# A chunked recurrence with a feed-forward block behind it: taking the four batches side by side

## The chip, the cores and the metric

The kernel runs on one core of a Trainium2 chip. A core has a matrix engine (TensorE, PE in the profile; its weight loads are listed apart as PEld), a vector engine (VectorE, DVE), a scalar engine (ScalarE, ACT), a general engine (GpSimd, POOL) and a sync engine (SyncE, SP), which here only issues DMAs. Each engine takes its own list of instructions; semaphores make one wait for another. The metric is the device time in microseconds of one execution. Lower is better.

## What is computed

```python
f = 1.0 / (1.0 + np.exp(-f_logit))              # B, H, S, D = 4, 8, 768, 48
state = np.zeros((B, H, D, D))
for t in range(S):
    state = f[:, :, t, :, None] * state + np.einsum('bhd,bhe->bhde', k[:, :, t], v[:, :, t])
    y[:, :, t] = np.einsum('bhd,bhde->bhe', q[:, :, t], state)
x = y.transpose(0, 2, 1, 3).reshape(B * S, H * D)   # 3072 x 384
a, b = x @ w1, x @ w2                                # w1, w2: 384 x 1024
out = (a * b @ w3) @ w_out                           # w3: 1024 x 1024, w_out: 1024 x 384
```

A gated linear recurrence runs over 768 tokens for each of 4 batches and 8 heads. Its output, with the heads side by side, goes through a feed-forward block whose hidden layer is the product of two projections. The four weight matrices come as 64-bit floats and have to be turned into 32-bit floats on the core.

## The kernel before

**The recurrence.** The tokens are cut into chunks of 128, so there are NU = 24 chunks, NCH = 6 for each batch. Two heads share the 112 used partitions (rows 0 to 47 and 64 to 111), and four such pairs (HP = 4) lie along the free axis. For a chunk u the function `front` loads q, k, the gate's logits and v, takes the sigmoid (`gates`, L518, ScalarE), and forms two running products of the gates on VectorE: `forward` (L526) and, after a reciprocal of the ends (L536), `backward` (L548). They scale q and k (`scale_q` L542, `scale_k` L556). `last` (L531) keeps the forward product's last column. Then, on TensorE, `turn` (L593) transposes the scaled k, copied to the tile kt by ScalarE (L727), and `pairs` forms the products of keys and queries. ScalarE copies them to the tile A (L700, L703), POOL zeroes what lies above the diagonal (`causal`, L709), `values` multiplies with v, and `update` forms the chunk's own contribution to the state from kt and v.

There are two forms. The first NPE = 2 chunks are taken whole: `pairs` with 128 by 128 blocks (L569), `first_values` (L607), and the contribution of the chunk before from a block-diagonal copy of the state (`blocks`, L834, and L613), and `first_update` (L625). All later chunks are cut into halves of 64 tokens: `pairs` with 64 by 64 blocks (L579), `values` (L653), `update` (L686). There a state in the middle, "mid", is wanted: `middle` adds the first half's contribution to the state S of the chunk before (L759), and the second half's to that (L762). `from_state` (L672) then multiplies q with S for the first half and with mid for the second. Before S is read by the next chunk, `state` scales it (L818, for the first two chunks L822 to L825) with G, the product of the chunk's last column and the next chunk's first gate, which POOL forms (`gains`, L809). A chunk that opens a batch (u = 0, 6, 12, 18) has no S to read, a chunk that closes one (5, 11, 17, 23) leaves out the second half of its update.

On TensorE the parts of a chunk are one task: for chunks 2 and 3 `begin` (pairs and update) and a "visit" (values and from_state); from chunk 4 on, the visit of u also holds pairs and update of u + 1. The output ys (L845) goes into the feed-forward block's input xt: for the first NPE chunks through TensorE (`moved`, L874) and ScalarE (L879), later with two DMAs through DRAM (yt, then xt: L866, L869).

**The weights.** `fetch` loads a piece of a matrix as pairs of 32-bit words into the tile "place" (L1396); ScalarE turns the lower words into a number (L1400), VectorE shifts the upper words (L1415), merges the two (L1419) and joins them (L1425). w1 and w2 come in four quarters, by the string EARLY = "23ACBD", which is the order on VectorE after chunk 1: chunks 2 and 3, then A (w1, first half of the hidden units), C (w1, second half), B (w2, first half) and D (w2, second half). Then come w_out and the rows of w3, and `fold` (L1464) forms w3 times w_out.

**The feed-forward block.** The tokens are taken in six blocks of 512, each of the four chunks 4n to 4n + 3. The first block's up projections (`part`, L897) run in groups of three matmuls over 256 tokens (six instructions in the trace); later blocks use a scheme with seven products instead of eight (`seven`, L993) or a longer one (`many`, L1148). `down` (L897 too, by a helper) multiplies with the folded weights and stores rows of the output (L1318). A line such as L897 is that of a helper that several parts call.

**What sets the order.** All of this is written as tasks with an engine, a cost, what they depend on, and a priority, into a `Plan`. `listed` takes, again and again, the task that can begin first by these costs, and the instructions are emitted in that order. So a changed dependency or a changed cost can move tasks on all engines and all DMA issues. `idle` (L399) puts matmuls on a constant tile where the plan expects TensorE to wait in the first 130 us. SP's list is in the plan too: a DMA that has to wait for its buffer holds back those behind it. The v tiles come from a pool of three (chunk 3 has a place of its own), so v of chunk 4 waits for chunk 0, v of chunk 5 for chunk 1.

The lines of the old kernel that the change touches most, the reading of the state:

```python
        for half in range(2):
            state = s["mid"] if half else st[u - 1].get("S")
            if state is None or half == 0 and u % NCH == 0:
                continue
```

Of the kernel before, what the change touches and what calls it, by code (L numbers as in the profile page):

```python
# [36 lines left out]
F32 = mybir.dt.float32  # L37
# [23 lines left out]
NPE = 2  # L61
# [226 lines left out]

def rows(par):
    return slice(64 * par, 64 * par + D)  # L290
# [3 lines left out]
def ranged(ctx, tc, q, k, f_logit, v, w1, w2, w3, w_out, out, ident, w12, wc, left):  # L294
# [30 lines left out]
    sb = [t[0:R, 0 : HP * R].rearrange("p (h r) -> p h r", r=R) for t in firsts]  # L325
# [80 lines left out]
    def setup():  # L406
# [21 lines left out]
        for t in sb:  # L428
            nc.vector.memset(t, 0.0)
# [43 lines left out]
    def loaded(dst, u):  # L473

        nc.sync.dma_start(dst, v[u])

    def front(u):
# [6 lines left out]
        def load(dst, src):  # L484
            def emit():
                if dst is fs[0] and u == 0:

                    nc.sync.dma_start(dst[0:64], src[u].rearrange("two d n -> (two d) n")[0:64])
                    nc.sync.dma_start(dst[rows(1)], src[u, 1])
                    return  # L490
                for par in range(2):
                    nc.sync.dma_start(dst[rows(par)], src[u, par])
            return emit
# [26 lines left out]
        t["g"] = plan.add("ACT", 0.65, gates, [t["lf"]] + past(u, 2, "r") + past(u, 3, "G"), n0)  # L520
        if u % NCH and "G" in tk[u - 1]:
            tk[u - 1]["G"]["deps"].append(t["g"])
# [75 lines left out]
    def first_values(u):  # L598

        s = st[u]  # L600
        opens = u % NCH == 0
        s["yb"] = bank().rearrange("p (h c) -> p h c", c=C)[0:R]
        for hp in range(HP):
            for par in range(2):
# [4 lines left out]
                    rhs=s["A"][:, par, hp], start=hp == 0, stop=opens, skip_group_check=True,  # L609
                )  # L610
        if not opens:
            for hp in range(HP):
                nc.tensor.matmul(  # L613
                    s["yb"][:, hp], lhsT=sb[(u - 1) % 2][:, hp], rhs=s["Q"][:, hp * C : hp * C + C],
                    start=False, stop=True, skip_group_check=True,
                )
# [44 lines left out]
    def from_state(u):  # L661

        s = st[u]
        for half in range(2):
            state = s["mid"] if half else st[u - 1].get("S")
            if state is None or half == 0 and u % NCH == 0:
                continue
# [9 lines left out]
    def update(u):  # L677
# [3 lines left out]
        for hp in range(HP):  # L681
            for half in range(1 if u % NCH == NCH - 1 else 2):
# [38 lines left out]
    def turning(u):  # L721
# [7 lines left out]
        if u < NPE:  # L729
            t["t"] = plan.add("PE", 0.45, lambda: turn(u), [t["k"]] + past(u, 1, "d"), need(u) - 999)  # L730
# [6 lines left out]
    def begin(u):  # L737

        def emit():
# [5 lines left out]
            "PE", 1.1, emit, [t["q"], t["k"], t["e"], t["lv"]] + past(u, 1, "m", "d"), need(u) - 999, slack=0.8,  # L745
# [3 lines left out]
    def middle(u):  # L749

        s, t = st[u], tk[u]
        opens, closes = u % NCH == 0, u % NCH == NCH - 1

        def emit():
            s["mid"] = mids[u % 2]
            if opens:
                nc.vector.tensor_copy(s["mid"], s["pd"][0])
            else:
                nc.vector.tensor_tensor(s["mid"], s["pd"][0], st[u - 1]["S"], ALU.add)  # L759
            if not closes:  # L760
                s["S"] = work.tile([R, HP, D], F32, name="S")
# [3 lines left out]
            "DVE", 0.36 if closes else 0.72, emit, [t["s"], t["m"]] + ([] if opens else past(u, 1, "d")) + past(u, 2, "v"), need(u) - 5,  # L765
        )

    def rest(u):
        s, t = st[u], tk[u]
        opens, closes = u % NCH == 0, u % NCH == NCH - 1  # L770
        n0 = need(u)
        if u < NPE:
# [5 lines left out]
                "PE", 1.05 if opens else 2.1, lambda: first_values(u), [t["c"], t["lv"]] + past(u, 1, "b"), n0 - 998,  # L778
                takes=["f"],
            )  # L780
            t["s"] = plan.add("PE", 0.6, lambda: first_update(u), [t["e"], t["lv"]] + past(u, 1, "d"), n0 - 997)
        else:
# [4 lines left out]
            def visit():  # L787
# [11 lines left out]
                [t["c"], t["lv"], t["mid"]] + past(u, 1, "y", *([] if opens else ["d"])) + [after[nm] for nm in ("q", "k", "e", "lv") if after],  # L799
# [6 lines left out]
        if not closes:  # L806
            def gains():
                s["G"] = work.tile([R, HP], F32, name="G")
                nc.gpsimd.tensor_tensor(s["G"], lasts[:, u], heads(gate[(u + 1) % 2][:, 0:NQ])[:, :, 0], ALU.mult)  # L809

            t["G"] = plan.add(
                "POOL", 0.3, gains, [t["l"]] + [tk[u + 1][nm] for nm in "g" if nm in tk[u + 1]] + past(u, 2, "d"), n0,
            )

            def state():
                gain = s["G"].unsqueeze(2).to_broadcast([R, HP, D])
                if u >= NPE:
                    nc.vector.tensor_tensor(s["S"], s["S"], gain, ALU.mult)  # L818
                    return
                s["S"] = work.tile([R, HP, D], F32, name="S")  # L820
                if opens:
                    nc.vector.tensor_tensor(s["S"], s["pd"], gain, ALU.mult)  # L822
                else:
                    nc.vector.tensor_tensor(s["S"], s["pd"], st[u - 1]["S"], ALU.add)
                    nc.vector.tensor_tensor(s["S"], s["S"], gain, ALU.mult)  # L825

            t["d"] = plan.add(
                "DVE", 0.36 if opens or u >= NPE else 0.72, state,
                [t["s"], t["G"]] + (past(u, 2, "b") if u < NPE else [t["mid"]]), n0, shared=True,
            )  # L830

            def blocks():
                for par in range(2):
                    nc.scalar.copy(sb[u % 2][rows(par), :, 64 * par : 64 * par + D], s["S"][rows(par)])  # L834

            if u + 1 < NPE:
                t["b"] = plan.add("ACT", 0.75, blocks, [t["d"]] + past(u, 1, "v"), n0)
# [23 lines left out]
        def written():  # L861

            s["yt"] = dram.tile([DM, C], F32, name="yt")
            for half in range(2):
                to = s["yt"][half * DH : half * DH + DH].rearrange("(b d) c -> d b c", d=D)
# [1145 lines left out]
```

## The time and the profile before

| | us |
|---|---|
| median of 3 runs (462.68 to 463.16) | 462.83 |
| the profiled execution | 464.25 |
| its span, from the first instruction to the last | 462.5 |
| ScalarE, GpSimd busy | 208.6, 63.9 |
| TensorE's granted clock over the span | 1.000 |

Engine busy time in stretches of the span (us; TensorE, weight loads, VectorE, ScalarE, GpSimd, and the mean busy share of the DMA engines):

| stretch | PE | PEld | DVE | ACT | POOL | DMA |
|---|---|---|---|---|---|---|
| 0 to 20 | 16.73 | 13.40 | 17.27 | 9.62 | 14.77 | 0.70 |
| 20 to 40 | 19.68 | 16.98 | 18.21 | 12.36 | 3.86 | 0.93 |
| 60 to 70 | 10.00 | 8.33 | 9.14 | 3.97 | 0.00 | 1.00 |
| 100 to 150 | 50.00 | 41.64 | 45.66 | 14.84 | 11.05 | 0.40 |
| 200 to 250 | 49.88 | 46.07 | 40.50 | 17.20 | 12.51 | 0.41 |
| 400 to 450 | 50.00 | 47.33 | 31.57 | 16.50 | 0.00 | 0.10 |

How to read it: a row of the timeline gives the start in the span, the duration, the engine, the line of the kernel, the operation, the tile that is written and those that are read, and in brackets how long the engine was idle before it and what ended that. "Waits" lists who waited for whom: total, times, longest. Busy TensorE time includes the filling matmuls of L399. Matmuls are pipelined and their ends are modelled, so the distance between starts says more than a duration.

### The profile page before, as it was taken

What the parts mean: (1) busy time and instruction counts of PE and PEld (TensorE: products, weight loads), DVE (VectorE), ACT (ScalarE), POOL (GpSimd) and SP (SyncE); (2) the same over time, 40 slices, a digit from 0 to 9 for tenths busy, and PEclk for the clock granted to TensorE, in tenths of its full rate; (3) what the DMA queues carried; (4) which work ended last, traced back from release to release, by engine and by line L of the source; (5) the groups of instructions that cost most, each with busy time, mean ns of one, the idle gap of its engine ahead of it and who ended that gap; (6) DMA issues with size and microseconds to landing.
All of it is one profiled execution on the core that took longest, in us unless ns stands there. A gap on an engine that the chain in (4) does not pass through costs nothing.

```text
span 462.5 us, 11749 instructions
## 1 busy us (share of the span) xinstructions
PE 452.9 (98%) x4800; PEld 395.5 (86%) x4800; DVE 362.1 (78%) x633; ACT 208.6 (45%) x468; POOL 63.9 (14%) x90
## 2 busy tenths in 40 slices
PE   7999999999999999999999999999999999999995
PEld 6788885666899888888998888998898988889995
DVE  8988899999898999988973599885658566768441
ACT  4565343432233553443323356566675666672000
POOL 9330000211223432223222000000000000000000
PEclk9999999999999999999999999999999999999999
DMA  6896997833246764447324337653265523200111
GB/s 181 272 331 206 336 353 254 267 104 103 70 125 178 213 185 125 111 124 191 102 55 114 112 94 216 201 157 125 95 184 170 192 69 96 89 1 0 35 69 39
DMA packets 43309, 68.75 MB, mean 149 GB/s; under 512 B 5217, under 2 KB 28386, under 8 KB 42226
## 3 DMA queue, kind: packets, MB, share of 16 engines
q1 hardware_dynamic: 43250, 67.95, 47.8%
q8 instruction: 39, 0.64, 0.6%
q14 instruction: 20, 0.16, 0.1%
HBM read 58.88 MB, written 9.04 MB: 147 GB/s over the span
## 4 chain that ended last, share of the span: by engine, by line
PE 94%; POOL 2%; DVE 2%; issue 0%; POOLq 0%; DVEq 0%
PE f L897 25%; PE f L993 15%; PE f L1148 11%; PE f L1464 9%; PE py L1148 6%; PE pa L1148 5%; PE py L897 4%; PE pa L897 4%; PE py L653 3%; PE pa L579 2%; PE pa L686 2%; PE f L593 2%; PE py L672 2%; PE py L993 1%; POOL ab L437 1%; PE f L399 1%
## 5 line engine op out<-in xcount | busy, mean ns | idle before, releaser
L709 POOL TENSOR_SCALAR_AFFINE_SELECT A<-A 64x512 f32<-64x512 f32 (+1 forms) x46 | 42.3, 920 | 110.6 <-ACT A L703 108.5
L1464 PE MATMUL f<-place 128*128 128x384 f32 x128 | 42.4, 487 | 0.0
L897 PE MATMUL f<-xt,w 128*128 128x256 f32 x192 | 42.1, 380 | 0.0
L897 PEld LDWEIGHTS f<-xt,w 128*128 128x128 f32 x192 | 36.3, 190 | 5.0
L1464 PEld LDWEIGHTS f<-place 128*128 128x128 f32 x128 | 23.9, 190 | 15.5
L993 PE MATMUL f<-xt,w 128*128 128x256 f32 x140 | 36.2, 380 | 0.0
L897 PE MATMUL f<-place 128*128 128x192 f32 x192 | 34.8, 327 | 0.0
L897 PEld LDWEIGHTS f<-place 128*128 128x128 f32 x192 | 31.5, 190 | 0.3 <-issue 0.2
L548 DVE TENSOR_TENSOR_SCAN bwd<-gate,back 112x512 f32<-112x512 f32 x24 | 30.4, 1268 | 0.7
L526 DVE TENSOR_TENSOR_SCAN fwd<-gate,floor 112x512 f32<-112x512 f32 x24 | 30.0, 1251 | 1.2 <-ACT gate L518 0.3
L993 PEld LDWEIGHTS f<-xt,w 128*128 128x128 f32 x140 | 26.3, 190 | 3.5
L845 ACT ACTIVATE ys<-py 112x512 f32<-112x512 f32 x22 | 13.1, 596 | 32.7 <-PE py L672 28.1
L1400 ACT ACTIVATE place<-place 128x512 f32<-128x512 uint32 (+2 forms) x24 | 21.3, 888 | 9.1 <-DMA place<-in_w_dram 7.9
L897 PE MATMUL f<-wc,ab 128*128 128x192 f32 x128 | 23.6, 328 | 0.0
L993 PE MATMUL f<-place 128*128 128x256 f32 x84 | 22.4, 385 | 0.0
L897 PEld LDWEIGHTS f<-wc,ab 128*128 128x128 f32 x128 | 21.3, 190 | 0.4
L518 ACT ACTIVATE gate<-f 112x512 f32<-112x512 f32 x22 | 13.9, 632 | 17.0 <-DMA f<-in_f_logit_dram 7.9
L809 POOL TENSOR_TENSOR G<-lasts,gate 112x4 f32<-112x4 f32 x20 | 11.0, 549 | 76.4 <-ACT lasts L531 30.4
L653 PEld LDWEIGHTS py<-A,vt 64*64 64x64 f32 (+1 forms) x672 | 13.3, 127 | 7.3 <-issue 6.5
L653 PE MATMUL py<-A,vt 64*64 64x64 f32 (+1 forms) x672 | 18.1, 223 | 0.2
L1540 ACT ACTIVATE A<-A,back 128x512 f32<-128x512 f32 x23 | 17.9, 778 | 0.2
L1262 DVE TENSOR_TENSOR place<-ab 128x512 f32<-128x512 f32 x24 | 16.5, 689 | 1.0 <-PE f L897 0.9
(355 smaller groups left out, 1045.6 us busy)
## 6 DMA issues: line engine op xcount, KB each, us to landing
place<-in_w_dram SPq DMA_DIRECT2D x21, 512.0 KB, 6.1
A<-in_w_dram SPq DMA_DIRECT2D x19, 512.0 KB, 4.1
place<-in_w_dram SPq DMA_DIRECT2D x8, 1024.0 KB, 5.9
q<-in_q_dram SPq DMA_DIRECT2D x46, 96.0 KB, 2.6
vt<-in_v_dram SPq DMA_DIRECT2D x23, 192.0 KB, 3.1
out_dram<-o SPq DMA_DIRECT2D x23, 192.0 KB, 2.1
k<-in_k_dram SPq DMA_DIRECT2D x44, 96.0 KB, 2.4
yt<-ys SPq DMA_DIRECT2D x44, 96.0 KB, 2.9
```

Source lines behind the costliest of these rows:

```text
L518: nc.scalar.activation(gate[u % 2][:, 0:NQ], fu, AF.Sigmoid)
L526: nc.vector.tensor_tensor_scan(s["P"], gate[u % 2][:, 0:NQ], floor, 0.0, ALU.mult, ALU.max)
L548: nc.vector.tensor_tensor_scan(s["R"][:, ::-1], gate[u % 2][:, NQ:0:-1], back[:, ::-1], 0.0, ALU.mult, ALU.max)
L653: done = nc.tensor.matmul(y_block(u, hp, par, half)[p0 : p0 + w], lhsT=s["v"][half * W : half * W + W, h * D : h * D + w], rhs=s["A"][half ...
L709: nc.gpsimd.affine_select(out=a, in_=a, pattern=pattern, compare_op=ALU.is_ge, fill=0.0, base=0, channel_multiplier=-1,)
L897: nc.tensor.matmul(out_, lhsT=lhs[i], rhs=rhs[i], start=start and i == 0, stop=i == len(lhs) - 1, skip_group_check=True,)
L993: nc.tensor.matmul(q[nm][:, which * TH : which * TH + TH], lhsT=lhs[i](which), rhs=rhs[i], start=start and which == 0 and i == 0, stop=i = ...
L1148: nc.tensor.matmul(banks[g, c][:, which * TH : which * TH + TH], lhsT=lhs, rhs=x_node(a), start=first and which == 0, stop=True, skip_grou ...
L1262: nc.vector.tensor_tensor(abs_[j], x, y, op)
L1400: nc.scalar.activation(part_.bitcast(F32), part_, AF.Copy, bias=2.0, scale=2.0**-51)
L1464: nc.tensor.matmul(w3s["p", jc], lhsT=w3s[jc][:, kc * P : kc * P + P], rhs=wos[:, kc], start=(kc == 0), stop=(kc == KF - 1),)
L1540: return lambda: nc.scalar.activation(a, a, AF.Sign, bias=small, accum_out=counts[:, i : i + 1])
```

## The change

The number u of a chunk no longer runs through one batch after the other. With `chunk(u) = u % B * NCH + u // B` the chunks 0 to 3 are the first of the four batches, 4 to 7 the second, and so on. The loads take `chunk(u)`, the stores take the rows that belong to it; a block of the feed-forward part now holds one chunk of each batch. So the state that chunk u reads is that of u - 4: five tiles for states go round (three of their own, two in unused columns of A), and G of u uses the gate of u + 4. The chunks that open a batch are 0 to 3, those that close one 20 to 23.

NPE becomes 4: the four opening chunks are all taken whole, so none has a state in the middle, at token 64. Since none of them reads a state, the block-diagonal copies with their clearing and the matmuls on them go. The contribution of an opening chunk is copied to its state by ScalarE (`saved`); the scaling of S, now the same for all chunks, waits for that copy. The number of chunks that go to xt through TensorE stays at two by a constant of its own, MOVED; chunks 2 and 3 go through DRAM as before, with the order of the heads in the whole form.

```diff
-NPE = 2
+NPE = 4
+MOVED = 2
...
+def chunk(u):
+
+    return u % B * NCH + u // B
...
-    sb = [t[0:R, 0 : HP * R].rearrange("p (h r) -> p h r", r=R) for t in firsts]
+    states = [keep.tile([R, HP, D], F32, name=f"S{i}") for i in range(3)]
+    states += [t[0:R, 2 * HP * W + HP * D : 2 * HP * W + 2 * HP * D].rearrange("p (h d) -> p h d", d=D) for t in flat]
...
-        for t in sb:
-            nc.vector.memset(t, 0.0)
...
-        nc.sync.dma_start(dst, v[u])
+        nc.sync.dma_start(dst, v[chunk(u)])
...
-        t["g"] = plan.add("ACT", 0.65, gates, [t["lf"]] + past(u, 2, "r") + past(u, 3, "G"), n0)
-        if u % NCH and "G" in tk[u - 1]:
-            tk[u - 1]["G"]["deps"].append(t["g"])
+        t["g"] = plan.add("ACT", 0.65, gates, [t["lf"]] + past(u, 2, "r") + past(u, B + 2, "G"), n0)
+        if u >= B and "G" in tk[u - B]:
+            tk[u - B]["G"]["deps"].append(t["g"])
...
-                    rhs=s["A"][:, par, hp], start=hp == 0, stop=opens, skip_group_check=True,
-                )
-        if not opens:
-            for hp in range(HP):
-                nc.tensor.matmul(
-                    s["yb"][:, hp], lhsT=sb[(u - 1) % 2][:, hp], rhs=s["Q"][:, hp * C : hp * C + C],
-                    start=False, stop=True, skip_group_check=True,
+                    rhs=s["A"][:, par, hp], start=hp == 0, stop=True, skip_group_check=True,
                 )
...
-            state = s["mid"] if half else st[u - 1].get("S")
-            if state is None or half == 0 and u % NCH == 0:
+            state = s["mid"] if half else st[u - B]["S"] if u >= B else None
+            if state is None:
                 continue
...
-        opens, closes = u % NCH == 0, u % NCH == NCH - 1
+        opens, closes = u < B, u + B >= NU
...
-                nc.vector.tensor_tensor(s["mid"], s["pd"][0], st[u - 1]["S"], ALU.add)
+                nc.vector.tensor_tensor(s["mid"], s["pd"][0], st[u - B]["S"], ALU.add)
             if not closes:
-                s["S"] = work.tile([R, HP, D], F32, name="S")
+                s["S"] = states[u % len(states)]
                 nc.vector.tensor_tensor(s["S"], s["pd"][1], s["mid"], ALU.add)
...
-                nc.gpsimd.tensor_tensor(s["G"], lasts[:, u], heads(gate[(u + 1) % 2][:, 0:NQ])[:, :, 0], ALU.mult)
+                nc.gpsimd.tensor_tensor(s["G"], lasts[:, u], heads(gate[(u + B) % 2][:, 0:NQ])[:, :, 0], ALU.mult)
...
+            if u < NPE:
+                def saved():
+                    s["S"] = states[u % len(states)]
+                    nc.scalar.copy(s["S"], s["pd"])
+
+                t["sc"] = plan.add("ACT", 0.33, saved, [t["s"]] + past(u, 1, "v"), n0)
+
             def state():
...
-            def blocks():
-                for par in range(2):
-                    nc.scalar.copy(sb[u % 2][rows(par), :, 64 * par : 64 * par + D], s["S"][rows(par)])
...
+                nc.vector.tensor_tensor(s["S"], s["S"], s["G"].unsqueeze(2).to_broadcast([R, HP, D]), ALU.mult)
+
+            t["d"] = plan.add("DVE", 0.36, state, [t["G"], t["sc" if u < NPE else "mid"]], need(u + B) if u + B < NU else n0, shared=True)
...
+                if u < NPE:
+                    to = s["yt"].rearrange("(b two d) c -> two d b c", two=2, d=D)[half]
...
-        if u < NPE:
+        if u < MOVED:
             t["z"] = plan.add("PE", 1.6, moved, [t["y"]], n0 - 996, takes=["f"], frees=[moving])
...
-                    t0 = n * TB + (i + half * UB // 2) * P
+                    t0 = ((i + half * UB // 2) * NCH + n) * P
```

## The prediction

> **What bounds the kernel.** I read the page's busy shares first, then the chain that ended last, then TensorE's own waits, and then the timeline of the first 40 us, because the first three leave only that stretch open. Busy shares and chain:
>
> ```profile
> PE 452.9 (98%) x4800; PEld 395.5 (86%) x4800; DVE 362.1 (78%) x633; ACT 208.6 (45%) x468; POOL 63.9 (14%) x90
> ...
> PE 94%; POOL 2%; DVE 2%; issue 0%; POOLq 0%; DVEq 0%
> ```
>
> TensorE is busy 98% of the span and makes 94% of the chain. All the waits of TensorE that the profile counts:
>
> ```profile
> PE f L399 <- DVE floor L422: 1.7, 1, 1.7
> PE py L593 <- DVE K L556: 0.9, 1, 0.9
> PE py L897 <- DVE ys L1192: 0.6, 1, 0.6
> PE f L593 <- DVE K L556: 0.4, 1, 0.4
> ```
>
> The reader is to see that no line names S, mid or G: TensorE never waits for a state. Reading a state four chunks later removes no TensorE wait; what can move the time is TensorE's amount of work and the moment from which it works without fillers. L399 (matmuls on a constant) fills the waits that the planner expects. The last fillers of the start and what ends them, VectorE's conversion of the first quarter of w1:
>
> ```profile
> 23.89 0.96 DVE L1415 TENSOR_SCALAR place<-place 128x1536 uint32<-128x1536 uint32 x1 [0.25 <-DMA place<-in_w_dram]
> ...
> 24.77 0.35 DVE L759 TENSOR_TENSOR A<-pa,S 112x192 f32<-112x192 f32 x1
> ...
> 25.15 0.36 DVE L762 TENSOR_TENSOR S<-pa,A 112x192 f32<-112x192 f32 x1
> ...
> 25.61 0.68 DVE L818 TENSOR_TENSOR S<-S,G 112x192 f32<-112x192 f32 x1
> ...
> 26.21 1.75 DVE L1419 SCALAR_TENSOR_TENSOR w<-place 128x1536 uint32<-128x1536 uint32 x1
> ...
> 27.99 1.76 DVE L1425 CUSTOM_DVE_ANT_0 w<-place,w 128x3072 uint16<-128x3072 uint16 x1
> ...
> 29.48 1.13 PE L399 MATMUL f<-floor 112*128 112x256 f32 x4
> ...
> 30.44 1.89 PE L897 MATMUL f<-xt,w 128*128 128x256 f32 x8
> ```
>
> The quarter lands at 23.89, three state operations of chunk 2 sit between its shift and its join, the join ends at 29.75, and the first up matmul starts at 30.44. From there to the last matmul, about 457, TensorE is full: 30.44 is what I call the start.
>
> **What the Trainium skill says.** "Perfetto Trace Analysis", Identifying the Most-Contended Engine, warns that matmul busy time is not a measure of headroom and points to the weight loads: here 86%, with gaps that belong to wide matmuls (L1464: 487 ns of matmul, 190 ns of load). Agreed, so I count starts, not busy time. "TensorE: Matmul & The Clock Gate", Architectural detail, says that ScalarE and VectorE run their queues strictly in order: a copy behind a blocked one waits; the trace's rows are in issue order throughout. "SBUF — State Buffer", Who interferes with whom, says a VectorE instruction with two SBUF inputs contends with a GpSimd one that reads SBUF. The trace agrees: K (L556) took 1.27 beside the mask (L709) against 0.69 alone, the scan (L526) 1.92 against 1.23.
>
> **Part 1: after the start (counts from the two instruction orders).** Before, chunk 3's visit came after the third up matmul group: L653 at 34.42, ups again at 35.80, so 1.38 of TensorE. Now all four first chunks are done ahead of the first up: -1.38. Added: chunks 6, 12 and 18 opened a batch and read no state at their first half; now all twenty later chunks read it, 8 matmuls more each. Such a set takes 0.23 (L672 at 35.25, the next set at 35.48): +3 x 0.23 = +0.69. The second half of an update, left out for a batch's last chunk, is left out four times either way (5, 11, 17, 23; now 20 to 23): 0. Fillers after the start: two groups' worth either way (2 matmuls, near 124): 0. Sum: -0.69. The edits of addresses (chunk(u) in loads, the output rows, the written layout of ys for chunks 2 and 3) keep counts and sizes: 0.
>
> **Part 2: the start itself.** Chunks 2 and 3 become whole-width: pairs 1.16 (L569) for 0.69 (L579), values 1.09 (L607) for 1.00 (L653) and two state sets, first update 0.67 for 0.62; gone are L613 (1.13), six fillers (0.43 each) and three state operations per chunk on VectorE. A copy of the update to S on ScalarE comes in: not in the trace at that size and place; nearest row, o<-pa 128x192, 0.32; I take 0.33 (between 0 if ScalarE idles and 1.3 for four in line).
>
> VectorE: to the backward scan of chunk 1 (end 11.72) nothing moves; the two memsets that go (0.91) lay under the wait for the first gate, which ends at 4.72. Then the wait for G (0.22) and S (0.36) go: K of chunk 1 starts 0.47 earlier. Later L824 and L825 go (20.38 to 21.10: 0.72). Chunk 3's Q would end at 23.64 - 0.47 - 0.72 = 22.45, or 23.05 with one more whole-width mask stretching it by 0.6. Both lie before the landing at 23.89, so the DMA takes over: shift 23.9 to 24.85, then L1419 at once to 26.6, L1425 to 28.4. With L759, L762 and L818 out of the way the join is 1.35 earlier.
>
> TensorE must by then have finished chunk 3, by its order. Worked forward with the durations above: turn 1 at 13.05 (K), values 0 to 14.75, pairs 1 to 15.9, update 1 to 16.6, moved 0 to 18.1 (1.52), pairs 2 to 19.3; ScalarE copies pairs 2 after chunk 3's lasts (scan stretched to about 19.6), 19.75 to 20.75; ys 1 to 21.55 (0.80); moved 1, behind two fillers, 21.8 to 23.3; pairs 3 to 24.5; ScalarE, with kt 2 and three raw-weight copies (0.69) in between, copies pairs 3 at 24.7 to 25.7, then ys 2 to 26.5, S 2 to 26.85; turn 3 to 27.65; the mask of chunk 3 ends about 27.0, values 3 to 28.75; kt 3, behind one raw-weight copy of the next quarter, to 28.25; update 3 to 29.4. So TensorE's own chain (29.45) and not the join (28.4 + 0.69 = 29.1) sets the new start: 0.99 earlier. Bounds: 29.1 if ScalarE has more room, 30.9 if two masks or copies stretch by 0.6 to 0.7 each.
>
> **Part 3: what is late next.** The SP queue is in order. Chunk 5's v load now stands ahead of all three loads of the second w1 quarter; it waits for chunk 1's values (about 20.4) instead of one of the three going at 17.20. Before, the other two went at 21.57, so the last of the three is not later. VectorE waited for that quarter until 30.59; if it lands as before: shift to 31.55, L1419 to 33.3, L1425 to 35.1 (before 36.03, with 0.70 of L759 and L762 and a stretched shift in it). Four up groups of 1.30 after 29.45 TensorE needs it at 34.65: wait 0.4 to 0.5 (0 if it lands at 29.2, 1.7 if its join stays at 36.03). The next quarter's shift stood at 36.06 and would end its join at 40.5 at the latest, needed at 29.45 + 8 x 1.30 + 0.45 = 40.3: about 0.1. The folds (L1464) come after 29 up groups, 67.6; their data were joined at 67.25 before. Turn 4 moves from behind the second fold (78.28) to behind the first (about 72.8); its K ended at 72.66 and VectorE has about 2 us less to do: covered. G, now waiting for the gate four chunks on, stands ahead of masks on POOL, but that gate also stands ahead of the masked copy on ScalarE: 0. Waits, together: +0.5.
>
> Sum: -0.99 - 0.69 + 0.5 = -1.2 (rounded). The profiled execution took 464.25 (span 462.5 and 1.75 around it), 1.42 above the median 462.83. So 463.05 profiled, 461.6 to 461.7 as a median; I say 461.7.
>
> **Rivals.** (a) The weight stream pins it. If the second quarter's join stays at 36.03 whatever VectorE sheds, the wait is 1.7 and the sum -0.99 - 0.69 + 1.7 = 0: 462.8. For it: DMA share is 0.93 from 20 to 40, and three loads sit behind one in-order wait. Against it: that join had 0.70 of state work in it.
>
> (b) The whole-width start is slower. TensorE may not begin an up before four chunks have gone through ScalarE and POOL in line: four copies of 1.00 (against two, and two of 0.58) and four masks of 1.09 to 1.59, with kt 3 behind a raw-weight copy that waits for a DMA. If that copy waits until about 29.5, kt 3 ends at 30.8, update 3 at 31.5, the start is 31.6, and with a further wait of 0.5 the time is +1.16 - 0.69 + 0.5 = +1.0: 463.8. It decides on the other side from a start of 32.1 (32.1 - 30.44 - 0.69 = +0.97) without further waits. Against it: the first two chunks do the same in the trace.
>
> (c) It does not do what it says for the time: states four chunks later cover nothing. That is part of the forecast, since no TensorE wait names a state.
>
> (d) The gain is larger: start at 29.1, no waits, and the 0.6 at L897 gone: -1.34 - 0.69 - 0.6 = -2.6: 460.2.
>
> **How the numbers follow.** Forecast 0.40, (d) and between 0.13; (a) 0.29; (b) 0.18, in which I count misplaced visits later on, where VectorE is 91% busy (45.7 of 50 us from 100 to 150). A measurement of this kernel tells about 0.2% (0.93 us) from no change: faster is below 461.9, slower above 463.8. Faster 0.53, same 0.29, slower 0.18. The range takes in (d) and most of (b): 460.1 to 464.0; the forecast's own is 461.0 to 462.4.
>
> **What shows it.** Right: the first up matmul between 29.1 and 30; no visit between ups; L1425 of the first quarter ending near 28.4; fillers 18 matmuls in place of 24. Wrong: a TensorE wait or filler gap before the fifth up group above 1 us (a); the first up after 32 behind kt and a DMA wait on ScalarE (b); TensorE waits of over 2 us in sum between 78 and 265, behind Q or K.

## The result, and the profile after

| | us |
|---|---|
| before, median of 10 runs beside it (462.68 to 463.35) | 462.95 |
| after, median of 10 runs (463.26 to 465.26) | 464.01 |
| ratio after / before, 95% interval | 1.0023 (1.0014 to 1.0033) |
| predicted (range 460.1 to 464.0) | 461.7 |
| profiled execution after, its span | 464.28, 462.5 |

The change made the kernel slower by about 1.1 us, where 1.2 less was forecast. The two profiled spans are equal (462.5), and that misleads: the last matmul starts at 457.69 after and 456.94 before, but from there to the end of the span the profiled execution before took 5.6 us, the one after 4.8. By the last matmul the changed kernel is 0.75 us later, by the medians 1.06; the spans do not stand for the medians. Lines of the new kernel are shifted: the up matmul L897 is L885, the fold L1464 is L1452, the fillers L399 are L406, the mask L709 is L707, K and Q (L556, L542) are L561 and L547, and the steps of the weights L1396, L1400, L1415, L1419, L1425 are L1384, L1388, L1403, L1407, L1413.

The page after: the busy shares, then the engines' shares of the chain that ended last.

```profile
PE 451.4 (98%) x4668; PEld 394.1 (85%) x4668; DVE 358.7 (78%) x626; ACT 208.9 (45%) x470; POOL 62.0 (13%) x88
...
PE 90%; DMA 4%; SPq 2%; DVE 1%; issue 1%; POOL 0%; ACT 0%; POOLq 0%; DVEq 0%; ACTq 0%
```

TensorE is busy 1.5 us less than before (452.9, fillers included), yet its share of the chain fell from 94% to 90%, SP's queue now has 2% and the DMAs 4%. The waits of TensorE (who waited for whom: total, times, longest) say where:

```profile
PE f L885 <- ACT place L1388: 1.7, 1, 1.7
PE f L406 <- DVE floor L429: 1.7, 1, 1.7
PE py L598 <- DVE K L561: 1.3, 1, 1.3
PE pa L574 <- DVE Q L547: 1.0, 1, 1.0
PE py L885 <- DVE ys L1180: 0.6, 1, 0.6
```

The first line is new, and it is larger than the loss: 1.7 us once, at an up matmul. The wait for Q of chunk 2 (1.0) is new too. The 1.3 for K is not the old 0.9 grown larger: the old one was for K of chunk 0 (at 8.38), this one is for K of chunk 1 (at 13.46). These two lie ahead of the first up matmul. As before, no line names a state. The wait of 1.7 in the timeline of VectorE and TensorE (start, duration, and in brackets the idle time before):

```profile
38.04 0.96 DVE L1403 TENSOR_SCALAR place<-place 128x1536 uint32<-128x1536 uint32 x1 [2.74 <-DMA place<-in_w_dram]
...
40.71 1.76 DVE L1413 CUSTOM_DVE_ANT_0 w<-place,w 128x3072 uint16<-128x3072 uint16 x1
...
42.62 3.69 PE L885 MATMUL f<-xt,w 128*128 128x256 f32 x16 [1.75 <-ACT place L1388]
```

VectorE stood idle 2.74 us before B's shift until the words had landed, the join L1413 ended at 42.47, and the ninth group of six up matmuls, the first that reads w2, began at 42.62. (The fifth group is the first that reads C. The expectations below say "fifth" of the wait for B; the ninth is meant.) The trace names ScalarE's raw copy (of a piece's lower words, L1388) as the releaser, but what the group reads is the tile that the join wrote 0.15 us before. In the profile before, B was joined at 40.81:

```profile
39.05 1.76 DVE L1425 CUSTOM_DVE_ANT_0 w<-place,w 128x3072 uint16<-128x3072 uint16 x1
```

The ninth group began at 42.38 there and waited for nothing: B had 1.57 us in hand.

SyncE's queue before (start, duration, line; place is a piece of weights, vt a chunk's v):

```profile
17.20 1.42 SPq L1396 DMA_DIRECT2D place<-in_w_dram  x1
21.19 0.33 SPq L475 DMA_DIRECT2D vt<-in_v_dram  x1
21.57 1.38 SPq L1396 DMA_DIRECT2D place<-in_w_dram  x3
27.91 0.33 SPq L475 DMA_DIRECT2D vt<-in_v_dram  x1
28.28 0.43 SPq L1396 DMA_DIRECT2D place<-in_w_dram  x1
...
29.95 1.01 SPq L1396 DMA_DIRECT2D place<-in_w_dram  x2
```

and after:

```profile
21.46 0.33 SPq L480 DMA_DIRECT2D vt<-in_v_dram  x1
21.84 1.37 SPq L1384 DMA_DIRECT2D place<-in_w_dram  x3
27.16 0.33 SPq L480 DMA_DIRECT2D vt<-in_v_dram  x1
...
28.50 2.12 SPq L1384 DMA_DIRECT2D place<-in_w_dram  x3
```

Before, one load of C left at 17.20, and v of chunk 5 (21.19) held back the two others and B's first, which all left at 21.57 to 22.5. After, v of chunk 5 (21.46) stands ahead of all of C, and v of chunk 6 (27.16) and the stores of yt ahead of all of B. B's last load leaves at nearly the same time in both (29.95 and 30.20), but it landed at 35.39 before and at 37.85 after. The DMA engines in two stretches (length, TensorE's busy time, clock, DMA share, GB/s), first before, then after:

```profile
20.00:28.00 8.00, 7.82 (x169) 1.00 0.99 380
28.00:38.00 10.00, 9.86 (x180) 1.00 0.89 290
```

```profile
20.00:28.00 8.00, 7.85 (x96) 1.00 0.82 276
28.00:38.00 10.00, 9.97 (x73) 1.00 0.91 301
```

From 20 to 28 us they moved 380 GB/s before and 276 after: 8 us x 104 GB/s = 0.83 MB, 2.2 us of their work at 380 GB/s, was left to be moved after 28. About 0.5 MB of that is B's own first load (512 KB), which left at 22.5 before and at 28.50 after.

### The profile page after: what moved, and what is told of

The parts are those of the page before. It is cut to its first block, busy times and chain, and to the rows that moved or that the text cites. A ratio compares the mean times of both kernels' runs of the same rounds, so it can differ in the third digit from the quotient of the medians.

```text
span 462.5 us, 11461 instructions
## 1 busy us (share of the span) xinstructions
PE 451.4 (98%) x4668; PEld 394.1 (85%) x4668; DVE 358.7 (78%) x626; ACT 208.9 (45%) x470; POOL 62.0 (13%) x88
## 4 chain that ended last, share of the span: by engine, by line
PE 90%; DMA 4%; SPq 2%; DVE 1%; issue 1%; POOL 0%; ACT 0%; POOLq 0%; DVEq 0%; ACTq 0%
PE f L885 23%; PE f L981 15%; PE f L1136 11%; PE f L1452 9%; PE py L1136 6%; PE pa L1136 5%; PE py L885 4%; PE pa L885 4%; DMA place<-in_w_dram 3%; PE py L651 3%; PE pa L584 2%; PE pa L684 2%; PE py L670 2%; PE f L598 2%; SPq L497 2%; PE py L981 1%
## 5 line engine op out<-in xcount | busy, mean ns | idle before, releaser
L707 POOL TENSOR_SCALAR_AFFINE_SELECT A<-A 64x512 f32<-64x512 f32 (+1 forms) x44 | 40.0, 909 | 100.9 <-ACT A L701 87.8
L885 PE MATMUL f<-xt,w 128*128 128x256 f32 x192 | 42.4, 381 | 1.8 <-ACT place L1388 1.7
L885 PEld LDWEIGHTS f<-xt,w 128*128 128x128 f32 x192 | 36.2, 190 | 7.4 <-ACT place L1388 2.1
L1452 PE MATMUL f<-place 128*128 128x384 f32 x128 | 42.4, 487 | 0.0
L1452 PEld LDWEIGHTS f<-place 128*128 128x128 f32 x128 | 23.9, 190 | 15.5
L885 PE MATMUL f<-place 128*128 128x192 f32 x192 | 35.3, 328 | 0.0
L885 PEld LDWEIGHTS f<-place 128*128 128x128 f32 x192 | 31.4, 190 | 0.4 <-issue 0.2
L1388 ACT ACTIVATE place<-place 128x512 f32<-128x512 uint32 (+2 forms) x24 | 21.1, 885 | 9.2 <-DMA place<-in_w_dram 6.8
L831 ACT ACTIVATE ys<-py 112x512 f32<-112x512 f32 x20 | 11.9, 597 | 28.3 <-PE py L670 27.2
L885 PE MATMUL f<-wc,ab 128*128 128x192 f32 x128 | 23.5, 327 | 0.0
L981 PE MATMUL f<-place 128*128 128x256 f32 x84 | 22.7, 385 | 0.0
L885 PEld LDWEIGHTS f<-wc,ab 128*128 128x128 f32 x128 | 21.3, 190 | 0.3
L651 PEld LDWEIGHTS py<-A,vt 64*48 64x48 f32 (+1 forms) x640 | 12.7, 127 | 6.9 <-issue 6.1
L547 DVE TENSOR_TENSOR Q<-q,fwd 112x512 f32<-112x512 f32 x23 | 17.5, 762 | 0.0
L651 PE MATMUL py<-A,vt 64*48 64x64 f32 (+1 forms) x640 | 17.2, 222 | 0.1
```

What stands on the lines that cost most here:

```text
L547: nc.vector.tensor_tensor(s["Q"], qu, s["P"], ALU.mult)
L651: done = nc.tensor.matmul(y_block(u, hp, par, half)[p0 : p0 + w], lhsT=s["v"][half * W : half * W + W, h * D : h * D + w], rhs=s["A"][half ...
L707: nc.gpsimd.affine_select(out=a, in_=a, pattern=pattern, compare_op=ALU.is_ge, fill=0.0, base=0, channel_multiplier=-1,)
L885: nc.tensor.matmul(out_, lhsT=lhs[i], rhs=rhs[i], start=start and i == 0, stop=i == len(lhs) - 1, skip_group_check=True,)
L981: nc.tensor.matmul(q[nm][:, which * TH : which * TH + TH], lhsT=lhs[i](which), rhs=rhs[i], start=start and which == 0 and i == 0, stop=i = ...
L1388: nc.scalar.activation(part_.bitcast(F32), part_, AF.Copy, bias=2.0, scale=2.0**-51)
```

## The experiments

The theory after the result, here "issue order": v of chunks 5 and 6, which wait for chunks 1 and 2, now stand in SyncE's queue where they hold C and B back, and B's late join costs the 1.7. Rivals: the new order of chunks as such is slower (whole-width start, VectorE), or what the plan made of later work. Each ratio is to the kernel before, run beside it on the same chip (its medians there were 463.35 to 463.43); the numbers in brackets are the ratio and its 95% interval.

**1 to 4: changing what the plan is told.** A plan task can be told not to begin before a given moment. The first experiment does that to the two loads of v in the changed kernel, the second in the kernel before:

```diff
-            ask[3],
+            ask[3], since=50.0 if u in (5, 6) else 0.0,
```

> The changed kernel, with the v loads of chunks 5 and 6 issued after the first w_out loads instead of ahead of the quarters C and B. Theory (issue order: on SP's in-order list these two loads wait for the values and updates of chunks 1 and 2 and hold back the weight loads behind them): the C loads go at about 17 instead of 21.8, B's last piece lands before 35 instead of 37.9, B is joined before 39.7, TensorE's wait of 1.7 us ahead of the first up group on B is gone, and the time falls by 1.2 to 1.9 us, to 462.1 to 462.8. Rival (bandwidth: the DMA engines carry the same bytes whatever the order): B's last piece still lands at 37 or later, the wait stays above 1 us, and the time stays at 463.6 to 464.2.

Measured: 462.46 (ratio 0.9981, 0.9973 to 0.9989), faster than before and 0.42% or 1.9 us below the changed kernel by the two ratios. B was joined at 40.29, somewhat later than I had put it, and no TensorE wait for B is left. One of 0.9 us, at 126 us, is new, so the plan did change other work as well.

> The kernel before, with the same two v loads moved back. Both theories: there B was joined 1.5 us ahead of its use, so TensorE has no wait to lose, and the time stays within 0.2% of 462.95. If it falls by more than 0.9 us, the order of the loads was worth something of its own, apart from the change.

Measured: 466.65 (1.0067, 1.0051 to 1.0084), not what was expected. B was joined earlier than before (39.39), and still 3 us were lost. TensorE's waits in it have four lines that the profile before has not, 2.1 us in sum, in the late feed-forward blocks (Q of L1148 is a piece of those). The largest:

```profile
PE py L1148 <- ACT Q L1169: 1.0, 2, 0.7
```

So telling the plan of a later load also made it order other work anew, and the time of such a variant does not isolate the load. That goes for the first experiment's gain too. The third takes chunks 2 and 3 in halves again, with the chunks side by side:

```diff
-NPE = 4
+NPE = 2
```

> The batches side by side, but NPE = 2: chunks 2 and 3 in halves with a state at token 64, as before. Theory (issue order): chunk 1 still reads no state, its values come as early, and the v load of chunk 5 stands ahead of C as in the changed kernel; the visit of chunk 3 is back among the up groups. Up groups start at 29.5 to 30.2, the wait for B stays at 0.5 to 1.5 us (the visit takes 1.4 of it), the time is 463.5 to 464.5. Rival (the four whole-width chunks are what costs): the start is earlier than 29.5 with no wait above 0.5, and the time is 462.0 to 462.8.

Measured: 465.32 (1.0041, 1.0027 to 1.0055), above what either theory had. TensorE:

```profile
28.83 2.86 PE L885 MATMUL f<-xt,w 128*128 128x256 f32 x12
...
41.91 3.26 PE L885 MATMUL f<-xt,w 128*128 128x256 f32 x14 [1.04 <-ACT place L1388]
```

The start is 1.2 us earlier than the changed kernel's, as the rival had it, but chunk 3's visit is back among the up groups (31.62 to 32.77, 1.15 us) and takes nearly all of that again. A wait for B is there (1.04), which the rival did not have, so the wait does not come from the whole-width form. The total says less: it contains late waits of 1.8 us in sum that the changed kernel has not. The fourth is the first with the weights' early loads free of the plan's limit on large transfers:

```diff
-            landed.append(moves(1, n, 400, load, held + list(deps), prio + 0.02 * i, SURE, lanes=("lane", "heavy")))
+            landed.append(moves(1, n, 400, load, held + list(deps), prio + 0.02 * i, SURE, lanes=("lane", "heavy") if prio > 0 else ("lane",)))
```

> The changed kernel with both v loads moved back and, besides, the twelve early weight loads listed without the plan's limit of three in flight, so that C and B follow A with nothing in between. Theory (issue order): all of C and B are issued by 20 and the DMA engines have no gap from 20 to 32; B's last piece lands by 33, no wait of TensorE for B; 462.0 to 462.6, at least as good as with the v loads moved alone. Rival (bandwidth): the pieces land no earlier than with the v loads moved alone, and A, whose pieces share the engines with more in flight, lands later than 23.5, so the start moves to 30.5 or later; 463.5 or more.

Measured: 471.34 (1.0177, 1.0148 to 1.0206), above what either theory had. The loads did what was wanted: all of C and B left by 22.7, B was joined at 38.90, and the first fold came at 65.12, 4.8 us ahead of the changed kernel's. More than that was lost later, in part in waits of the late blocks: TensorE's L1136, which is the L1148 of before, waited 1.5 us once for Q (VectorE, L1180). The profiled execution (468.73) is the fastest of the six (468.73 to 473.64), so its waits don't show the whole loss. Where the rest went was not followed.

**5 to 7: moving the two issues and nothing else.** The plan is left as it is, and only its finished list is changed, so that every engine but SyncE keeps its order:

```diff
-    for t in plan.order():
+    order = plan.order()
+    v5, v6 = (tk[u]["lv"]["deps"][0] for u in (5, 6))
+    order.remove(v5)
+    order.remove(v6)
+    i = order.index(asked[8]["deps"][0]) + 1
+    order[i:i] = [v5, v6]
+    for t in order:
```

Here asked[8] is B's last load. The sixth is the same in the kernel before; the seventh puts the two, in the kernel before, where the changed kernel has them (ahead of asked[3], C's first, and asked[6], B's first).

> The changed kernel with nothing replanned: every engine keeps its order, and only the two SyncE instructions that load v of chunks 5 and 6 are moved, to just behind the last load of B. Issue-order theory: B's three loads no longer stand behind loads that wait for chunks 1 and 2, B is joined by 40.6 instead of 42.47, no TensorE wait before the fifth up group is left over 0.3 us, and the time is 1.5 to 2.1 us below the changed kernel's 464.0: 461.9 to 462.5. Rival (the gain of the first experiment came from what its new plan did to other work): less than 0.5 us below, 463.5 to 464.0, although B is joined earlier.

Measured: 462.27 (462.00 to 462.86; ratio 0.9975, 0.9967 to 0.9983). Against the changed kernel's 1.0023 that is 0.48% or 2.2 us, a little more than expected. SyncE, TensorE and VectorE:

```profile
17.14 2.12 SPq L1384 DMA_DIRECT2D place<-in_w_dram  x3
...
28.44 1.43 SPq L1384 DMA_DIRECT2D place<-in_w_dram  x3
29.97 1.00 SPq L480 DMA_DIRECT2D vt<-in_v_dram  x2
...
35.67 10.70 PE L885 MATMUL f<-xt,w 128*128 128x256 f32 x48
...
38.84 1.76 DVE L1413 CUSTOM_DVE_ANT_0 w<-place,w 128x3072 uint16<-128x3072 uint16 x1
```

C leaves at 17.14 in one go, B's join ends at 38.84 + 1.76 = 40.60, and the up matmuls run on from 35.67 past the ninth group without a gap. The gain is somewhat more than the wait of 1.75; the rest was not traced. This kernel is faster than before by 1.1 us, the fastest of the versions that compute the same; the intervals of the first and the ninth overlap its own.

> The kernel before with the same two instructions moved behind the last load of B, and nothing replanned. TensorE had no wait for C or B there, so by the issue-order theory nothing is gained: 462.6 to 463.3. If late loads of v themselves cost the 3 us that the second experiment lost, it is 465.5 or more; if that loss came from the new plan, it is not seen here and the time is the kernel before's.

Measured: 463.25 (1.0007, 0.9997 to 1.0018): nothing, as issue order has it. Late loads of v as such do not cost the 3 us of the second experiment, so by elimination the new plan does (though the second's two loads left later still, at 47 us, the sixth's at 30.6 and 31.4). Which of the reordered tasks lost them was not followed further.

> The kernel before with the two instructions put where the changed kernel has them: v of chunk 5 ahead of C's first load, v of chunk 6 ahead of B's first. Issue-order theory: B's loads leave from about 27.9 on, B is joined at about 42.3, TensorE waits 1.4 to 2.0 us before the fifth up group, and the time is 464.3 to 465.0. Rival (the wait belongs to the chunks' new order, not to the queue's): no such wait, 462.6 to 463.3.

Measured: 464.94 (1.0038, 1.0017 to 1.0059): the expected size, at another place; the wait before the ninth group did not come. B was joined at 41.57, 0.76 later than before, and nothing waited for it: in the kernel before, chunk 3's visit lies among the first up groups (34.32 to 35.70 here, 1.38), and the ninth group began at 42.28. Without the visit it would have been due at about 40.9 (42.28 - 1.38). By the times, the loads' delay ran on to the folds instead, of which the third pair waited:

```profile
80.11 5.43 PE L1464 MATMUL f<-place 128*128 128x384 f32 x16 [0.86 <-DVE place L1425]
```

It started at 80.11 against 78.99 before, and two folds later the lag was 1.6, which is the loss by the medians (1.5). So the visit that the change takes out was also the cover of B's join. With the visit, the same queue costs its time 40 us later.

**9 and 10: which of the two loads.** As the fifth, with one of them moved. In the expectations, theory C blames chunk 5's load ahead of C, theory V chunk 6's load ahead of B.

> The fifth experiment with only v of chunk 5 moved behind B's last load; v of chunk 6 stays ahead of B's first. Theory C (the wait on chunk 1 sends C's three loads out 5 us late, and their 1.5 MB then meet B's in the DMA engines): most of the gain stays, B is joined by 41.0, TensorE's wait before the fifth up group is at most 0.5 us, 462.2 to 462.9. Theory V (the 192 KB of v of chunk 6 and its wait on chunk 2, just ahead of B, are what delays B): the wait stays 1.1 us or more and the time is 463.2 to 464.0.

Measured: 462.42 (0.9978, 0.9968 to 0.9988). SyncE and TensorE:

```profile
21.46 0.33 SPq L480 DMA_DIRECT2D vt<-in_v_dram  x1
...
29.37 1.41 SPq L1384 DMA_DIRECT2D place<-in_w_dram  x3
...
41.52 5.85 PE L885 MATMUL f<-xt,w 128*128 128x256 f32 x26 [0.83 <-DVE w L1413]
```

> The fifth experiment with only v of chunk 6 moved behind B's last load; v of chunk 5 stays ahead of C's first, so C leaves at about 21.8. Theory C: the wait before the fifth up group stays 1.1 us or more, B joined at 41.6 or later, 463.2 to 464.0. Theory V: B is joined by 41.0, a wait of at most 0.5 us, 462.2 to 462.9.

Measured: 463.66 (1.0008, 0.9991 to 1.0024). TensorE:

```profile
36.42 5.42 PE L885 MATMUL f<-xt,w 128*128 128x256 f32 x24 [0.48 <-DVE w L1413]
43.16 4.12 PE L885 MATMUL f<-xt,w 128*128 128x256 f32 x18 [1.32 <-DVE w L1413]
```

By the times it is chunk 5's load: moved alone it brings nearly all of the fifth experiment's gain. Chunk 6's alone brings about a third by the ratios (1.0023 to 1.0008), but the intervals overlap, and the trace (of an execution 0.78 above the median) shows nothing of it: C is late as well (0.48 before the fifth group), B was joined at 43.02, and its wait is 1.32. The trace of the ninth shows a larger wait than I had allowed, 0.83 with B's join at 41.37. There the stores of yt stood ahead of B until 29.3, 0.9 later than in the fifth; the profiled execution took 462.85, 0.43 above the median.

The ninth is not quite what its expectation says. The tiles for v are given out in the order of issue, so with chunk 5's load moved behind it, chunk 6's load took the place that chunk 1 leaves: it went at 21.46 and not at 27.16, and its wait for chunk 2 was not tested there. The tenth takes that wait away, and B's first load leaves hardly earlier (28.25 for 28.50), since the stores of yt stand there anyway. The two together also separate B's own issue from the bytes ahead of it. In the ninth B's last load left at 30.35 and landed at 36.87, with C gone early; in the tenth it left at 29.92 and landed at 38.51, with C late.

**8, 11 and 12: the start.** The prediction had the first up matmul at 29.45, the trace has 30.05. The timeline after, with GpSimd's masks (POOL L707) beside VectorE:

```profile
11.68 1.09 POOL L707 TENSOR_SCALAR_AFFINE_SELECT A<-A 128x1024 f32<-128x1024 f32 x1
11.74 1.57 DVE L561 TENSOR_TENSOR K<-k,bwd 112x512 f32<-112x512 f32 x1
...
17.37 1.17 POOL L707 TENSOR_SCALAR_AFFINE_SELECT A<-A 128x1024 f32<-128x1024 f32 x1 [4.61 <-ACT A L698]
17.51 1.57 DVE L547 TENSOR_TENSOR Q<-q,fwd 112x512 f32<-112x512 f32 x1
...
19.23 1.16 PE L574 MATMUL pa<-Q,K 48*128 48x128 f32 x16 [0.96 <-DVE Q L547]
...
25.66 1.77 DVE L1407 SCALAR_TENSOR_TENSOR w<-place 128x1536 uint32<-128x1536 uint32 x1 [0.87 <-ACT place L1388]
...
26.84 1.55 POOL L707 TENSOR_SCALAR_AFFINE_SELECT A<-A 128x1024 f32<-128x1024 f32 x1 [4.07 <-ACT A L698]
...
27.47 2.53 DVE L1413 CUSTOM_DVE_ANT_0 w<-place,w 128x3072 uint16<-128x3072 uint16 x1
...
30.05 1.13 PE L885 MATMUL f<-xt,w 128*128 128x256 f32 x4
```

K of chunk 1 was to start 0.47 earlier for want of the wait for G. It did (11.74 for 12.21), but the mask of chunk 0 began at 11.68, and K ended at 13.31, 0.17 earlier. Q of chunk 2 began 0.14 behind the mask of chunk 1 and took 1.57 instead of 0.68, and pairs 2 (PE pa) began at 19.23, predicted 18.1. Before, Q had begun 0.04 ahead of that mask: the mask took longer, and only the scan of chunk 3 behind it (18.32) was stretched:

```profile
17.54 0.68 DVE L542 TENSOR_TENSOR Q<-q,fwd 112x512 f32<-112x512 f32 x1
17.58 1.59 POOL L709 TENSOR_SCALAR_AFFINE_SELECT A<-A 128x1024 f32<-128x1024 f32 x1 [0.69 <-ACT A L700]
```

So a mask that came 0.2 us earlier (17.37) changed which of the two had to wait. The join of A took 2.53 instead of 1.76, and the merge ahead of it had stood 0.87 for ScalarE's third raw copy, which lay behind the copy of xt. The eighth takes up this last point: as the fifth, with that raw copy ahead of the copy of xt, so that the join can start earlier.

```diff
...
+    copy = tk[1]["x"]
+    order.remove(copy)
+    order.insert(order.index(lows[2]) + 1, copy)
...
```

> The fifth experiment's kernel, and besides ScalarE's third copy of A's raw words is put ahead of the xt copy of chunk 1, which is needed only at the first up matmul. Theory A (that copy delayed A's merge by 0.87 us and with it the first up matmul): A's merge starts 0.6 to 0.9 us earlier, the first up matmul at 29.3 to 29.7 instead of 30.05, and the time is 0.3 to 0.7 us below the fifth experiment's. Theory B (join and mask share their time anyway, and TensorE's own chain through the mask of chunk 3 ends at 30.0): the merge starts earlier, the first up matmul stays within 0.2 us of 30.05, and the time is the fifth experiment's within 0.3 us.

Measured: 462.76 (0.9986, 0.9972 to 1.0001), not better than the fifth.

```profile
26.59 1.76 DVE L1414 CUSTOM_DVE_ANT_0 w<-place,w 128x3072 uint16<-128x3072 uint16 x1
28.38 1.73 DVE L1404 TENSOR_SCALAR place<-place 128x1536 uint32<-128x1536 uint32 x1
...
26.92 2.38 POOL L707 TENSOR_SCALAR_AFFINE_SELECT A<-A 128x1024 f32<-128x1024 f32 x1 [4.05 <-ACT A L698]
...
29.35 1.09 PE L611 MATMUL f<-A,place 128*64 128x128 f32 x16 [0.70 <-POOL A L707]
...
30.82 1.35 PE L885 MATMUL f<-xt,w 128*128 128x256 f32 x5
```

The join did start a microsecond earlier and took 1.76. But it was now ahead of the mask of chunk 3 (26.92), and that took 2.38 instead of 1.55, so that values 3 waited 0.70 and the first up matmul came at 30.82, later than the fifth's 30.17. Neither theory had it quite so: they do not share their time, one waits for the other. The eleventh leaves out the mask of chunk 1, the twelfth those of chunks 0 to 3 (with `u < NPE` in the condition). What lies above the diagonal then stays in and the output is not the wanted one, so these two are for the time alone:

```diff
         def causal():
+            if u == 1:
+                return
```

> The fifth experiment's kernel with GpSimd's mask of chunk 1 left out (so chunk 1's upper triangle stays in; nothing else changes). Lock theory (a VectorE operation with two inputs and that mask shut each other out, so that Q of chunk 2 took 1.57 us instead of 0.68 and sent pairs 2 and all behind it back by a microsecond): Q of chunk 2 takes 0.7, the wait of TensorE for Q falls from 1.0 to under 0.3, and the first up matmul stands at 28.9 to 29.5 instead of 30.17. Rival (the start is set by the weight words of A and their conversion): first up within 0.3 of 30.17. The total time gains less than the start, since B's join at 40.6 is then needed at about 40: 461.4 to 462.2.

Measured: 461.48 (0.9966, 0.9954 to 0.9979). The up matmul's helper is L888 here.

```profile
17.50 0.69 DVE L547 TENSOR_TENSOR Q<-q,fwd 112x512 f32<-112x512 f32 x1
...
29.16 17.20 PE L888 MATMUL f<-xt,w 128*128 128x256 f32 x77
```

> The same with the masks of chunks 0 to 3 all left out. Lock theory: besides, K of chunk 1 takes 0.7 instead of 1.6, TensorE's wait for it falls from 1.0 to about 0.2, the join of A takes 1.76 instead of 2.53, and the first up matmul stands at 28.1 to 28.9. Rival: first up at 29.8 or later. Total 461.2 to 462.2, with a wait for B left.

Measured: 461.24 (0.9959, 0.9945 to 0.9973).

```profile
25.88 1.76 DVE L1416 CUSTOM_DVE_ANT_0 w<-place,w 128x3072 uint16<-128x3072 uint16 x1
...
28.36 10.63 PE L888 MATMUL f<-xt,w 128*128 128x256 f32 x48
39.28 6.93 PE L888 MATMUL f<-xt,w 128*128 128x256 f32 x31 [0.29 <-DVE w L1416]
```

One mask is worth 1.01 us of the start (30.17 to 29.16), all four 1.81 (to 28.36). The last matmul moved by 0.88 and 1.46 (454.93 and 454.35 for 455.81); by the ratios alone the two are not clear of the fifth, the intervals overlap. With the one mask gone Q of chunk 2 took 0.69 and pairs 2 began at 18.34; with all gone the join took 1.76, and TensorE's wait for K of chunk 1 was 0.44, not 0.2. B was not missed as much as I expected (0.29 in the twelfth), because its loads stand behind the stores of chunk 2's output, and these came earlier along with the start (B's first load at 27.41 and 26.96, for 28.44).

## Why the prediction was wrong

| trace | first up | last matmul | between | wait for B |
|---|---|---|---|---|
| before | 30.44 | 456.94 | 426.50 | 0 |
| after | 30.05 | 457.69 | 427.64 | 1.75 |
| 5, issues late | 30.17 | 455.81 | 425.64 | 0 |

**Part 1 (-0.69) was right in size.** Between the first up and the last matmul the changed kernel differs from the one before by 427.64 - 1.75 - 426.50 = -0.61 without its new wait, the fifth experiment by -0.86. These are single traces: the sixth experiment, TensorE's order as before, has 426.08 for the 426.50, so 0.4 is not to be read here. The visit among the ups is gone as forecast; the two terms of the sum were not measured singly. States read four chunks later uncovered nothing: no TensorE wait names a state in any of these traces.

**Part 2 (-0.99) was mis-sized: -0.39.** The step that failed is that VectorE runs through from K of chunk 1, with one more mask costing 0.6. "K of chunk 1 starts 0.47 earlier" gained 0.17, since it ran into a mask; the mask of chunk 1 met Q of chunk 2, which TensorE waits for, where before it met the scan of chunk 3, for which it does not. "Pairs 2 to 19.3" ended at 20.4, pairs 3 at 25.6 for 24.5, update 3 at 30.0 for 29.4. The eleventh experiment shows that this one meeting cost 1.0. A's join, "L1425 to 28.4", ended at 30.00: 0.87 for the raw copy behind xt and 0.77 beside the mask. So TensorE's own chain, which the prediction took for the limit, and the join ended within 0.02 us of each other; starting the join earlier (eighth) only handed the wait to the mask, and so to the chain. The prediction's own bound of 30.9 for masks and copies that stretch covers the 30.05; its sum did not.

**Part 3 (+0.5) is where the sign was lost.** The quarter that I feared was C, and it was joined at 35.30 against a forecast of 35.1. For the next quarter, B, I wrote "would end its join at 40.5 at the latest", needed at 40.3; it was 42.47, needed at 40.9, and TensorE waited 1.75. The need came about 1.5 us earlier than before (40.9 for 42.38), and that the prediction had; the join came 1.66 later (42.47 for 40.81), and that it had not. So the step that failed is "The next quarter's shift stood at 36.06": B's landing was taken as before, with no reason given, and its late landing was put at nothing. The argument for C, "the last of the three is not later", held nearly as it stands: C's last load landed at 30.76 for 30.47 before. But it says nothing of what C's three loads, leaving together, and v of chunk 6 do to B behind them: I left out what else those DMA engines then had to move. C left 4.6 us later for its first load, B's own first load 6.0 later, 0.83 MB fell behind, and B's last load landed 2.5 us later with its issue time nearly unchanged. The fifth experiment shows that the place of the two loads of v in the queue costs the wait, the ninth and tenth that it is mostly chunk 5's load. That it acts through the bytes that are still to be moved is read from the landing times of the ninth and tenth (36.87 and 38.51); no run varies the bytes alone. Rival (a) had the right kind of event, the weight stream pinning the start, but at the wrong quarter, and its sum of 0 did not have the smaller gain of the start. (By the prediction's own 34.65 its wait would have been 36.03 - 34.65 = 1.4, not 1.7.)

Together: -0.39 - 0.61 + 1.75 = +0.75 by the traces, +1.06 by the medians; the other 0.3 is not accounted for. Without the queue's part the change would have been worth what was forecast (-1.1 in the fifth experiment, -1.2 predicted), though in part by chance: a start that gained less than forecast, and no wait where 0.5 was put in.

## What to carry to other kernels

When a change moves a waiting DMA ahead of others in an in-order queue, don't stop at the issue times: sum the bytes that are not moved while the queue stands, and ask which load, two or three behind, will pay for them. A piece of work taken out of a critical engine may be the cover of something late just behind it; here a visit of 1.38 us had hidden B's join. Where a plan orders the work, test one instruction's place in the finished list, since nearly the same wish told to the plan cost 3 us, with new waits more than 200 us later. And where two engines shut each other out, a start that moves by 0.2 us can decide which of them waits; ask for each such pair which one the critical engine waits for.

## What was not expected of the hardware

In these traces a VectorE operation with two inputs and GpSimd's mask do not slow each other; by their ends, one stands until the other is done. K of chunk 1, Q of chunk 2 and K of chunk 3 each ended 0.54 to 0.55 us after the mask that they met (12.77, 18.54, and 22.78 in the trace after), whatever their overlap, against 0.68 to 0.69 for one alone. It holds the other way round: in the eighth experiment the join ended at 28.35 and the mask, begun at 26.92, at 29.30, 0.95 later, against 1.09 for one alone. The shift, which has one input only, was held too: L1404 in the eighth took 1.73 instead of 0.95 and ended at 30.11, 0.81 after the mask. The merge L1407 does the same: it ended at 27.43 after, and the mask that began in its shade at 28.39, 0.96 later. The prediction quoted the Trainium skill for contention only; its page "SBUF — State Buffer", Who interferes with whom, says more: "only the shared port pair causes contention, and it's an exclusive lock". The runs agree. A cost of "a mask stretches it by 0.6" is therefore no constant: it is what is left of the mask (or of the other operation) when the two meet, and which of them pays depends on who came first.
